# Four edits of hand-set order in a Fourier-mixing and ELU kernel: sums, products and a copy of the last step, and the steps of six sums per batch

## The chip, the core and the metric

The kernel runs on one core of a Trainium2 chip. The metric is the device time of one execution in microseconds (us); lower is better. The engines are TensorE (PE, matrix products; PEld is its weight load), VectorE (DVE), ScalarE (ACT), GpSimd (POOL) and SyncE (SP, which issues DMAs). Each engine works through its own queue in order, and engines wait for one another by semaphores.

## The reference

A two-dimensional Fourier transform of each batch, of which the real part goes through a two-layer network with an ELU between the layers.

```python
x: (8, 3008, 256) float32              # attention input
X = np.fft.fft(x, axis=1)
X = np.fft.fft(X, axis=2)
h = X.real.reshape(24064, 256) @ w_in  # w_in (256, 2048)
g = np.where(h > 0.0, h, np.exp(np.minimum(h, 0.0)) - 1.0)
out = g @ w_out                        # w_out (2048, 256), out (24064, 256)
```

## The kernel before

The transform over the rows is done on TensorE with constant cosine and sine matrices; the transform over the channels is folded into the first weight matrix. Because of the symmetry of the spectrum only half of the rows of each batch (1504) are transformed, as a cosine part (`Rr`) and a sine part (`Ir`); the sum and the difference of their products with the folded weights (`Wc` and `Ws`, both in `Wsc`) give a row and its mirror row. The 8 x 1504 = 12032 columns are cut into 47 tiles of 256 columns, each tile into 8 **steps** over the hidden width: 376 steps, 0 to 375. All data are float32; each product of the code (`mm`, L590) appears as two MATMUL instructions.

**One step** i does this. `mm_P` (PE, `H<-Rr,Wsc`) makes the cosine product in a PSUM bank `H`. `even_part` (DVE, L1339) reads it into `E`. `mm_Q` (PE, `H<-Ir,Wsc`) then adds the sine product into the same bank, so it has to wait for `even_part`. `h_minus` (DVE, L1353) makes the mirror row from `E` and `H`. `below_plus`, `below_minus`, `exp_plus`, `exp_minus` (ACT) and `g_plus`, `g_minus` (DVE, L1369) make the ELU: the results are blocks 0 and 1 (from `g_minus`) and 2 and 3 (from `g_plus`) of the buffer `G`. Four sums on POOL (L601), in this order, then make the operands of a seven-product scheme for the second layer: `sum_1` (block 5 = 2 - 3), `sum_3` (4 = 2 - 0), `sum_2` (2 = 5 - 0), `sum_4` (6 = 2 + 1). The second layer is `mm_X1` (`pA` from block 0; `pB` from block 1; then `pB` from the new block 2, with weights `WT`), `mm_X2` (`pC` from blocks 4 and 5) and `mm_X3` (`pD` from blocks 3 and 6).

**The order is written out by hand.** Each piece of work is entered with a due time (`at(t, fn)`, L1662). Slot k begins at k*T with T = 4.8 (`PERIOD`); the entries are sorted by due time and issued in that order, which is then the order of each engine's queue (`pin` keeps it). The due times are not times on the chip. Within a slot PE runs P of step k, X1 of step k-2, Q of step k, X2 and X3 of step k-2. In the first step of a tile X3 comes at the start of the following slot.

**Transforms of later batches** go in between: for batches b = 2 to 7, all entries of `rel(step, dt, ...)` (L1997) fall in slot r0 + step with r0 = 48*b - 70. `quarter_pairs` and `shift_pairs` (DVE) make sums and differences of row groups that the DFT products (`at_quarter`, L1968: two halves of products, `H<-QM,...`) take. `shift_pairs(b, ri, kodd, k)` (L876) issues two DVE instructions of 94x128 elements: with kodd = 1 two SCALAR_TENSOR_TENSOR (through `turn`, L870), with kodd = 0 two TENSOR_TENSOR (L598), all with both tensor inputs in SBUF. Their due time is 4.25 within the slot, which puts them behind `h_minus` and ahead of the `even_part` of the next slot on DVE.

**The last tile** (46) is combined from `pA` to `pD` on DVE in pieces: `comb_1` (u from `pA`, `pB`), a transpose, `comb_2` and `comb_22` (v and u with `pC`), a transpose, `comb_half` 0 (v with `pD`), a transpose, `comb_half` 1, a transpose. After each of the four transposes (L1527) `store` issues four DMAs of the result, two on the SP queue and two on the ACT queue (L1569). **The middle rows** (row 1504 of each batch) are done by themselves at the end: `mid_out` (PE, 16 small products, `H<-w,mid`), `mid_copy` (L1615, to SBUF), `mid_pick` (PE, one product that sums four groups), `mid_store` (DVE copy L1624 and one DMA on SP).

Of the kernel before, what the change touches and what calls it, by code (L numbers as in the profile page):

```python
# [15 lines left out]
ALU = mybir.AluOpType  # L16

SEQ = 3008
ND = 256
# [156 lines left out]
def kernel(  # L176
# [7 lines left out]
    nc = tc.nc  # L184
# [3 lines left out]
    n_tiles = (n_cols + TW - 1) // TW  # L188
# [17 lines left out]
    pin = tc.keep_in_program_order  # L206
# [393 lines left out]
    def gtt(o, a, b, op):  # L600
        pin(nc.gpsimd.tensor_tensor(out=o, in0=a, in1=b, op=op))  # L601

    def act(o, i, func=AF.Copy, **kw):
        pin(nc.scalar.activation(out=o, in_=i, func=func, **kw))  # L604
# [682 lines left out]
    def spread_ext(b, kodd):  # L1287
        for sl, a, z in ring_cut(b * HALF + kodd * RUN, RUN, False):
            a, z = a + kodd * RUN, z + kodd * RUN
            nc.sync.dma_start(  # L1290
                out=Rb[:, sl],
                in_=r128_dr[b : b + 1, a:z].to_broadcast([128, z - a]),
            )
            nc.sync.dma_start(out=Ir[127:128, sl], in_=r128_dr[b : b + 1, a:z])
# [68 lines left out]
    def exp_neg(ap):  # L1363
        act(ap, ap, func=AF.Exp, scale=-1.0)
# [33 lines left out]
    def blk(S, j, n=1):  # L1398
        return S.G[:, j * TW : (j + n) * TW]

    def sum_1(i):
        S = steps[i]
        gtt(blk(S, 5), blk(S, 2), blk(S, 3), ALU.subtract)

    def sum_3(i):
        S = steps[i]
        gtt(blk(S, 4), blk(S, 2), blk(S, 0), ALU.subtract)

    def sum_2(i):
        S = steps[i]  # L1410
        gtt(blk(S, 2), blk(S, 5), blk(S, 0), ALU.subtract)

    def sum_4(i):
        S = steps[i]
        gtt(blk(S, 6), blk(S, 2), blk(S, 1), ALU.add)

    def prod(i, a, half, lhsT, j):
        S, T = steps[i], tiles[i // 8]
# [18 lines left out]
    def mm_plain(i, a):  # L1437

        S = steps[i]
        q = i // 8  # L1440
        if i % 8 == 0 and a == 0:
            tiles[q] = Tile()
            tiles[q].acc = [bank(t) for t in ACC[2 * q : 2 * q + 2]]
        for n, (half, sign) in enumerate(((0, a), (1, 1 - a))):
            for r in range(2):
                mm(
                    tiles[q].acc[a][:, n * TW : (n + 1) * TW],
                    w2b(i, r, half),
                    blk(S, 2 * sign + r),
                    i % 8 == 0 and n == 0 and r == 0,  # L1450
                    i % 8 == 7,
                )
        if a:
            del steps[i]
# [158 lines left out]
            )  # L1613

    def mid_copy():  # L1615
        pin(nc.vector.tensor_copy(out=state["mh"][:, 0:ND], in_=state["mo"][:, 0:ND]))

    def mid_pick():
        po = state["mo"] = bank("H")
# [14 lines left out]
    state = {}  # L1634
# [27 lines left out]
    def at(t, fn):  # L1662
        events.append((t, len(events), fn))
# [69 lines left out]
    for slot in range(8):  # L1733
        i = slot % 2 * 8 + slot // 2
# [56 lines left out]
    T = PERIOD  # L1791
# [27 lines left out]
    for i in range(8):  # L1819
        at((12.9 + 0.5 * i) * T + 3.6, lambda i=i: sum_weights(i))  # L1820
    total = n_tiles * 8
    WINOGRAD = (
        (T + 2.91, sum_1),
        (T + 3.6, sum_3),
        (T + 4.4, sum_2),
# [4 lines left out]
    for slot in range(total):  # L1830
        i = slot % 2 * 8 + slot // 2 if slot < 16 else slot
        t = slot * T

        X3 = ((3 * T + 0.1 if i % 8 == 0 else 2 * T + 3.05, "", mm_X3),)
        for dt, key, fn in (
            (0.0, "P", mm_P),
            (0.9, "V", even_part),
            (2.17, "Q", mm_Q),
            (3.55, "h", h_minus),
            (4.2, "b+", below_plus),  # L1840
            (4.8, "b-", below_minus),
            (T + 0.01 if slot < 16 else T + 1.5, "x+", exp_plus),
            (T + 0.02 if slot < 16 else T + 2.21, "x-", exp_minus),
            (T + 2.2, "g+", g_plus),
            (T + 2.9, "g-", g_minus),
        ) + (
            (
                (2 * T + 0.87, "Xa", lambda i: mm_plain(i, 0)),
                (2 * T + 3.04, "Xb", lambda i: mm_plain(i, 1)),
            )  # L1850
            if i < 16
            else tuple((dt, "", fn) for dt, fn in WINOGRAD) + X3
        ):
            if f"{key}{slot}" not in front:
                at(t + dt, lambda fn=fn, i=i: fn(i))
# [28 lines left out]
    def safe(col):  # L1884

        return 8 * ((col - 1 - RING) // TW) + 8 if col > RING else 0
# [81 lines left out]
    def at_quarter(step, b, ri, kodd, finish, join):  # L1968
        box = []

        def d():
            if not box:
                box.append(Quarter(ri, b, kodd, state["Q", ri, kodd, b]))
            return box[0]

        def half(par):
            d().ps = bank("H")
            d().mms(par, d().ps)

        at(step * T + 4.75, lambda: half(0))  # L1980
        at((step + 1) * T + 0.9, lambda: d().copy())
        at((step + 1) * T + 1.0, lambda: d().unfold())
        at((step + 2) * T + 4.75, lambda: half(1))
        if kodd:
            at(finish * T + 4.26, lambda: d().finish())
            at((step + 3) * T + 0.9, lambda: d().copy_odd())
            at((step + 3) * T + 1.0, lambda: d().unfold_odd())
        assert join + 1 >= safe(b * HALF + (kodd + 1) * RUN)
        t = join * T + (4.25 if kodd else 1.01)
        at(t, lambda: d().plus())  # L1990
        at(t + 0.001, lambda: d().minus())

    for b in range(2, NB):
        s0 = (b - 1) * steps_b
        r0 = 48 * b - 70

        def rel(step, dt, fn, *key):  # L1997
            at((r0 + step) * T + dt, lambda: fn(*key))

        for far, rows in (  # L2000
            (0, ((0, 2, 0.2), (1, 2, 1.3), (3, 3, 0.2), (2, 5 if b == 2 else 3, 1.3))),
            (1, ((0, 27, 1.3), (1, 25, 0.2), (3, 28, 1.3), (2, 26, 3.0))),
        ):
            for j, n, dt in rows:
                rel(n, dt, load_quarter, b, j, far)
        for j, far, n, dt in (
            (0, 0, 4, 0.2), (3, 0, 4, 1.3), (1, 0, 5, 0.2), (2, 0, 6 if b == 2 else 5, 3.1),
            (1, 1, 27, 1.4), (2, 1, 28, 0.2), (0, 1, 29, 0.2), (3, 1, 30, 0.2),
        ):
            rel(n, dt, load_odd, b, j, far)  # L2010
        rel(4, 3.0, quarter_row, b)
        for far, start in ((0, 6), (1, 30)):
            for n in range(8):
                rel(start + n, 1.3, mirror_sum, (0, 3)[n % 2], far, (0, 2, 1, 3)[n // 2])
        for step, *key in (
            (13, 0, 0, 0), (20, 1, 0, 0), (21, 0, 0, 1), (22, 1, 0, 1),
            (35, 0, 1, 0), (36, 1, 1, 0), (37, 1, 1, 1), (38, 0, 1, 1),
        ):
            rel(step, 4.25, half_sum, *key)
        for step, *key in (  # L2020
            (14, 0, 0, 0), (21, 1, 0, 0), (23, 0, 0, 1), (25, 1, 0, 1),
            (38, 0, 1, 0), (40, 1, 1, 0), (42, 1, 1, 1), (44, 0, 1, 1),
        ):
            for ri in range(2):
                rel(step + ri, 1.3, channel_fold, ri, *key)
            kodd, far, h = key
            if h:
                rel(step, 4.0, channel_edge, kodd, far)
        for n in range(4):
            ri, m = divmod(n, 2)  # L2030
            rel(46 + n, 1.3, quarter_pairs, b, ri, 0, 1 + m)
        for n, step in enumerate((43, 44, 45, 46, 51, 53)):
            ri, m = divmod(n, 3)
            rel(step, 4.25, quarter_pairs, b, ri, 1, (2, 1, 3)[m])
        for step, *key in (
            (48, 0, 0, "u"), (49, 0, 1, "v"), (50, 1, 0, "v"), (52, 0, 1, "u"),
            (54, 1, 1, "u"), (56, 1, 1, "v"),
        ):
            rel(step, 4.25, shift_pairs, b, *key)
        for step, ri, kodd, finish, join in (  # L2040
            (51, 0, 0, 0, 54),
            (56, 1, 0, 0, 59),
            (59, 0, 1, 60, 75),
            (64, 1, 1, 66, 76),
        ):
            at_quarter(r0 + step, b, ri, kodd, r0 + finish, r0 + join)
        for kodd in range(2):
            step = s0 + (28, 38)[kodd]
            assert step >= safe(b * HALF + (kodd + 1) * RUN)
            at(step * T + 1.0, lambda b=b, kodd=kodd: spread_ext(b, kodd))  # L2050
# [5 lines left out]
    for n, dt, fn in (  # L2056
        (last, 4.75, mid_mm),
        (last + 1, 1.46, mid_below),
        (last + 2, 1.6, lambda: exp_neg(state["mr"])),
        (last + 3, 1.0, mid_g),  # L2060
        (total + 1, 3.3, mid_out),
        (total + 2, 2.9, mid_copy),
        (total + 2, 2.91, mid_pick),
        (total + 2, 2.92, mid_store),
    ):
        at(n * T + dt, fn)
# [32 lines left out]
```

## Time and profile before

| | |
|---|---|
| median of 3 runs | 1912.35 us (1911.55 to 1912.51) |
| profiled execution, its own time | 1911.92 us |
| span of the profiled execution, first to last instruction | 1910.1 us |
| granted TensorE clock | 1.000 |
| MATMUL instructions | 8972 |
| DVE, ACT, POOL busy | 1466.7, 876.9, 1352.6 us |

The profiled execution's time is 1.8 us more than its span, and 0.43 us below the median. A timeline line is: start, duration, engine, line of the kernel, operation, output<-inputs, shape, count, and in brackets the idle time before it with what ended it. The times of a merged line run from the first start to the last end. A queue's name ends in q (SPq, ACTq). A MATMUL lasts longer than the distance to the next one, since they are pipelined: two MATMULs of 128x256 start 0.216 us apart when nothing holds them, and 22 of them, a plain step, take 4.75 us.

### The profile page before, as it was taken

How to read it: one execution, taken by the hardware profiler on the slowest of the kernel's cores; microseconds unless marked ns; L12 is line 12 of the kernel's file. 1: busy time of each engine (PE TensorE's matmuls, PEld its weight loads, DVE VectorE, ACT ScalarE, POOL GpSimd, SP SyncE). 2: the span in 40 equal slices, each digit the busy share in tenths (PEclk: the TensorE clock that was granted, in tenths of full speed). 3: DMA queues.
4: the chain of work that ended last, by engine and by line, in shares of the span. 5: the costliest groups of instructions: out<-in, count | busy, mean ns of one | idle time of the engine just before them, and what ended most of it. 6: DMA issues, size and time to landing. Idle time of an engine off the chain costs nothing.

```text
span 1910.1 us, 27916 instructions
## 1 busy us (share of the span) xinstructions
PE 1901.3 (100%) x8972; PEld 1648.8 (86%) x8972; DVE 1466.7 (77%) x2786; ACT 876.9 (46%) x1710; POOL 1352.6 (71%) x1837
## 2 busy tenths in 40 slices
PE   9999999999999999999999999999999999999999
PEld 6888888888888888888888888888888888888887
DVE  8766667887778887778877787777877778767666
ACT  5754444444444444444444444444444444444443
POOL 4888667776677766777667776687766777556665
PEclk9999999999999999999999999999999999999999
DMA  8145212111011110111102111022110210000101
GB/s 339 45 33 43 57 24 47 50 25 35 12 45 41 32 33 12 46 40 30 31 19 49 35 27 29 13 55 44 24 24 16 55 20 16 17 12 15 20 12 23
DMA packets 278934, 73.80 MB, mean 39 GB/s; under 512 B 254402, under 2 KB 268998, under 8 KB 278788
## 3 DMA queue, kind: packets, MB, share of 16 engines
q1 hardware_dynamic: 270148, 61.58, 16.0%
q0 software_dynamic: 6464, 10.18, 1.7%
q8 instruction: 71, 1.16, 0.3%
q14 instruction: 75, 0.61, 0.1%
q10 hardware_dynamic: 2176, 0.26, 0.1%
HBM read 47.10 MB, written 24.80 MB: 38 GB/s over the span
## 4 chain that ended last, share of the span: by engine, by line
PE 96%; DVE 2%; DMA 0%; issue 0%; ACT 0%; POOL 0%; POOLq 0%; DVEq 0%
PE H L592 38%; PE pB L592 17%; PE pC L592 17%; PE pD L592 17%; PE pA L592 9%; DMA xl<-in_x_dram,ix 0%; DVE E L1339 0%; DVE e L689 0%; DVE o L689 0%; POOL w L601 0%; DVE G L1369 0%; DVE e L870 0%; DVE G L1353 0%; DVE Rr L598 0%; DVE pow L460 0%
## 5 line engine op out<-in xcount | busy, mean ns | idle before, releaser
L601 POOL TENSOR_TENSOR G<-G 128x256 f32<-128x256 f32 x1440 | 1049.3, 738 | 505.5 <-DVE G L1369 349.8
L604 ACT ACTIVATE G<-H 128x512 f32<-128x512 f32 x376 | 224.6, 597 | 931.5 <-DVE G L1353 927.9
L1339 DVE SCALAR_TENSOR_TENSOR E<-Rb,wex,H 128x256 f32<-128x256 f32 x752 | 327.5, 476 | 337.3 <-PE H L592 331.4
L592 PE MATMUL H<-Ir,Wsc 128*128 128x256 f32 x1504 | 388.1, 380 | 1.1 <-DVE E L1339 1.0
L592 PE MATMUL H<-Rr,Wsc 128*128 128x256 f32 x1504 | 387.6, 380 | 0.5 <-ACT Wsc L604 0.5
L592 PE MATMUL pC<-G,WT 128*128 128x256 f32 x1440 | 369.5, 379 | 0.0
L592 PEld LDWEIGHTS H<-Ir,Wsc 128*128 128x128 f32 x1504 | 277.7, 189 | 52.1 <-DVE E L1339 7.5
L592 PEld LDWEIGHTS H<-Rr,Wsc 128*128 128x128 f32 x1504 | 282.1, 190 | 41.6 <-issue 2.3
L592 PEld LDWEIGHTS pC<-G,WT 128*128 128x128 f32 x1440 | 273.6, 190 | 37.2
L1353 DVE SCALAR_TENSOR_TENSOR G<-E,H 128x512 f32<-128x512 f32 x376 | 257.0, 684 | 44.7 <-POOL G L601 11.4
L1369 DVE SCALAR_TENSOR_TENSOR G<-G,H 128x512 f32<-128x512 f32 x376 | 255.8, 680 | 37.9 <-ACT G L604 37.5
L1369 DVE SCALAR_TENSOR_TENSOR G<-M,G 128x512 f32<-128x512 f32 x376 | 256.7, 683 | 0.8 <-ACT M L604 0.8
L604 ACT ACTIVATE G<-G 128x512 f32<-128x512 f32 x376 | 233.3, 621 | 0.0
L592 PE MATMUL pB<-G,w 128*128 128x256 f32 x784 | 229.3, 379 | 0.0
L592 PE MATMUL pA<-G,w 128*128 128x256 f32 x784 | 229.3, 379 | 0.0
L592 PE MATMUL pD<-G,w 128*128 128x256 f32 x784 | 229.2, 379 | 0.0
L604 ACT ACTIVATE M<-G 128x512 f32<-128x512 f32 x376 | 223.9, 596 | 2.8 <-DVE G L1353 2.8
L604 ACT ACTIVATE M<-M 128x512 f32<-128x512 f32 x376 | 221.1, 588 | 0.1
L592 PE MATMUL pB<-G,WT 128*128 128x256 f32 x720 | 214.4, 379 | 0.0
L592 PE MATMUL pD<-G,WT 128*128 128x256 f32 x720 | 214.1, 379 | 0.0
L592 PEld LDWEIGHTS pA<-G,w 128*128 128x128 f32 x784 | 148.9, 190 | 20.5
L592 PEld LDWEIGHTS pB<-G,w 128*128 128x128 f32 x784 | 148.9, 190 | 20.4 <-PE H L592 0.2
(172 smaller groups left out, 1555.0 us busy)
## 6 DMA issues: line engine op xcount, KB each, us to landing
out_dram<-ot SPq DMA_DIRECT2D x496, 32.0 KB
xq<-in_x_dram SPq DMA_DIRECT2D x48, 94.0 KB
out_dram<-ot SPq DMA_DIRECT2D x256, 2.0 KB
Rb<-r SPq DMA_DIRECT2D x10, 376.0 KB
raw<-in_moe_w_in_dram SPq DMA_DIRECT2D x7, 512.0 KB
MC<-dft_mats SPq DMA_DIRECT2D x3, 943.5 KB
xq<-in_x_dram SPq DMA_DIRECT2D x12, 192.0 KB
xq<-in_x_dram SPq DMA_DIRECT2D x36, 64.0 KB
```

Of the source, the lines that this page charges most:

```text
L592: nc.tensor.matmul(out_, lhsT=lhsT, rhs=rhs, start=start, stop=stop, skip_group_check=True)
L601: pin(nc.gpsimd.tensor_tensor(out=o, in0=a, in1=b, op=op))
L604: pin(nc.scalar.activation(out=o, in_=i, func=func, **kw))
L1339: nc.vector.scalar_tensor_tensor(out=S.E[:, c], in0=Rb[:, cols(i)], scalar=wex[:, f : f + 1], in1=S.H[:, c], op0=ALU.mult, op1=ALU.add,)
L1353: nc.vector.scalar_tensor_tensor(out=two(S.G[:, 0:512])[:, :, ::-1], in0=two(S.E), scalar=2.0, in1=two(S.H), op0=ALU.mult, op1=ALU.subtract,)
L1369: nc.vector.scalar_tensor_tensor(out=o, in0=e, scalar=-1.0, in1=h, op0=ALU.add, op1=ALU.max)
```

## The change

Four edits.

1. In the last step (375) `sum_3`, `sum_2` and `sum_4` are put on VectorE; `sum_1` stays on GpSimd.
2. X3 of the last but one step (374) is put later: behind X2 of step 375 and ahead of X3 of step 375. The order of PE's second-layer products at the end was X1 X2 X3 (374), X1 X2 X3 (375) and becomes X1 X2 (374), X1 X2 (375), X3 (374), X3 (375).
3. The first copy of the middle rows is put on ScalarE, and its due time from 2.9 to 2.75. The transposes of the last tile are due at 2.4, 2.6 and 2.8 of the same slot, so that the copy now stands ahead of the last transpose and of its stores.
4. Four of the six `shift_pairs` entries of each batch from 2 to 7 are put in other slots, and with that change places: (0,1,u) from 52 to 50, (1,0,v) from 50 to 56, (1,1,u) from 54 to 58, (1,1,v) from 56 to 64.

```diff
+    def tt_of(i):
+
+        return vtt if i == n_tiles * 8 - 1 else gtt
+
...
     def sum_3(i):
         S = steps[i]
-        gtt(blk(S, 4), blk(S, 2), blk(S, 0), ALU.subtract)
+        tt_of(i)(blk(S, 4), blk(S, 2), blk(S, 0), ALU.subtract)
 
     def sum_2(i):
         S = steps[i]
-        gtt(blk(S, 2), blk(S, 5), blk(S, 0), ALU.subtract)
+        tt_of(i)(blk(S, 2), blk(S, 5), blk(S, 0), ALU.subtract)
 
     def sum_4(i):
         S = steps[i]
-        gtt(blk(S, 6), blk(S, 2), blk(S, 1), ALU.add)
+        tt_of(i)(blk(S, 6), blk(S, 2), blk(S, 1), ALU.add)
...
     def mid_copy():
-        pin(nc.vector.tensor_copy(out=state["mh"][:, 0:ND], in_=state["mo"][:, 0:ND]))
+        act(state["mh"][:, 0:ND], state["mo"][:, 0:ND])
...
-        X3 = ((3 * T + 0.1 if i % 8 == 0 else 2 * T + 3.05, "", mm_X3),)
+        X3 = (
+            (
+                3 * T + 0.1 if i % 8 == 0 else 3 * T + 3.045 if i == total - 2 else 2 * T + 3.05,
+                "",
+                mm_X3,
+            ),
+        )
...
         for step, *key in (
-            (48, 0, 0, "u"), (49, 0, 1, "v"), (50, 1, 0, "v"), (52, 0, 1, "u"),
-            (54, 1, 1, "u"), (56, 1, 1, "v"),
+            (48, 0, 0, "u"), (49, 0, 1, "v"), (50, 0, 1, "u"),
+            (56, 1, 0, "v"), (58, 1, 1, "u"), (64, 1, 1, "v"),
         ):
             rel(step, 4.25, shift_pairs, b, *key)
...
         (total + 1, 3.3, mid_out),
-        (total + 2, 2.9, mid_copy),
+        (total + 2, 2.75, mid_copy),
         (total + 2, 2.91, mid_pick),
         (total + 2, 2.92, mid_store),
```

## Prediction

> **What bounds the kernel now.** I read the engines' busy times first, then what PE's weight loads waited for, then the timeline of one batch's slots, then that of the end.
>
> ```profile
> PE 1901.3 (100%) x8972; PEld 1648.8 (86%) x8972; DVE 1466.7 (77%) x2786; ACT 876.9 (46%) x1710; POOL 1352.6 (71%) x1837
> ```
>
> PE is the bound over the whole span, so a shorter sum on another engine is worth nothing unless PE waited for it or it stands behind PE's last product. PE's own waits as the waits view counts them are small, but a busy MATMUL can hide a stall. Those of the weight loads show where to look:
>
> ```profile
> PEld H L592 <- DVE E L1339: 7.5, 19, 1.1
> ...
> PEld pB L592 <- POOL G L601: 0.8, 3, 0.4
> ```
>
> The first line is Q waiting for `even_part`, 19 times. To find what PE really lost I took the distance from each P product's start to the next (the length of a slot) over the whole run. It is 4.75 us in plain slots, and nearly everywhere a slot is longer by the DFT products in it alone. Two slots of each later batch are not. Here are slots r0+53 to r0+55 and r0+58 of batch 5 (r0 = 170), from the PE timeline:
>
> ```profile
> 1144.75 1.03 PE L592 MATMUL H<-Rr,Wsc 128*128 128x256 f32 x4
> ...
> 1150.77 1.03 PE L592 MATMUL H<-Rr,Wsc 128*128 128x256 f32 x4
> 1155.52 1.03 PE L592 MATMUL H<-Rr,Wsc 128*128 128x256 f32 x4
> 1160.59 1.03 PE L592 MATMUL H<-Rr,Wsc 128*128 128x256 f32 x4
> ```
> ```profile
> 1170.98 1.03 PE L592 MATMUL H<-Rr,Wsc 128*128 128x256 f32 x4
> ...
> 1176.81 1.03 PE L592 MATMUL H<-Rr,Wsc 128*128 128x256 f32 x4
> ```
>
> Slot 223 (r0+53) takes 6.02, slot 228 (r0+58) 5.83 with DFT products of the same shapes: 0.19 lost. Slot 225 (r0+55) has no DFT product and takes 5.07, not 4.75: 0.32 lost. Why, in slot 225:
>
> ```profile
> 1155.65 1.40 DVE L870 SCALAR_TENSOR_TENSOR e<-o,twist_tab,e 94x128 f32<-94x128 f32 x2
> 1156.98 0.85 DVE L1339 SCALAR_TENSOR_TENSOR E<-Rb,wex,H 128x256 f32<-128x256 f32 x2
> 1157.89 0.73 PEld L592 LDWEIGHTS H<-Ir,Wsc 128*128 128x128 f32 x4 [0.45 <-DVE E L1339]
> ```
>
> A scalar pair (`shift_pairs`) ends 1.53 us into the slot, `even_part` starts at 1.46, Q waits. The same happens in slot 223 (`even_part` at 1.33). In undisturbed slots it starts at 1.06 to 1.10, and at 1.14 (slot 220) PE still loses nothing. So the stall is the start of `even_part` less 1.14: 0.32 and 0.19, as found.
>
> The end of the run:
>
> ```profile
> 1898.46 0.68 DVE L1369 SCALAR_TENSOR_TENSOR G<-M,G 128x512 f32<-128x512 f32 x1
> 1898.69 3.02 POOL L601 TENSOR_TENSOR G<-G 128x256 f32<-128x256 f32 x4 [0.80 <-DVE G L1369]
> ...
> 1900.96 0.30 PEld L592 LDWEIGHTS pB<-G,WT 128*128 128x128 f32 x2 [0.37 <-POOL G L601]
> ...
> 1901.77 0.69 DVE L598 TENSOR_TENSOR u<-p,pB 128x512 f32<-128x512 f32 x1 [2.62 <-PE pB L592]
> ...
> 1905.93 0.39 DVE L1616 COPY mid<-H 128x256 f32<-128x256 f32 x1
> 1906.37 0.14 PEld L592 LDWEIGHTS H<-mid,pick 128*32 128x32 f32 x2 [1.61 <-DVE mid L1616]
> 1907.03 0.41 DVE L1624 COPY mid<-H 8x256 f32<-8x256 f32 x1 [0.71 <-PE H L592]
> 1907.47 0.29 SPq L1625 DMA_DIRECT2D out_dram<-mid  x1
> ```
>
> PE waits for the third sum of step 375; DVE starts the last tile when the third product of X1 is done and is then busy without a gap to the middle copy at 1905.93, although `mid_out` was done at 1905.25. That copy leads to the last DMA, which lands at 1908.91; the span ends 1.23 later with the closing waits.
>
> **What the Trainium skill says.** SBUF — State Buffer, Who interferes with whom: a VectorE instruction with two SBUF inputs contends with a GpSimd instruction that reads SBUF, the lock is exclusive for the whole instruction, and the first to start has it. The trace agrees: a pair's second instruction starts at 0.44 in slot 220 while a POOL sum runs from 0.34 to 1.07, and ends at 1.21, 0.14 after that sum. VectorE: DVE Perf Modes, "The TRN2 errata — SBUF-src ops pay a fixed extra latency per instruction": a float32 tensor_tensor of N elements takes (N+151)/0.96 ns, so 424 ns at 256; the trace has 422 (e<-xl 128x256, nothing on POOL). DMA: Bandwidth & Descriptors, Issuing engines are not separate DMA queues: several issuing engines save only the sequencer's time of issue. Here a store occupies the ACT queue for 0.44 (median), which counts for edit 3.
>
> **The change part by part.** *Scalar pairs (edit 4).* No instruction is added. The six batches' lengths of slot r0+53 are 6.018, 6.022, 6.026, 6.020, 6.020, 6.025 against 5.833: 1.13 us over. Those of r0+55 are 4.935, 4.939, 5.068, 5.065, 4.935, 4.941 against 4.749: 1.39 over (the 5.07s are batches whose joins wrap in the ring buffer, two DVE pieces more). Sum 2.52. The pairs due in 52 and 54 ran at the head of 53 and 55; both go. Nothing else is late there: in slot 52 `h_minus` ends at 4.87 of 4.78, in slot 54 at 4.97 of 4.75, so `even_part` then waits for P alone, at about 1.06.
>
> Where they land. Slot 50 loses a TENSOR_TENSOR pair and gets a scalar pair. The nearest row is the scalar pair due in 49: it starts at 4.5, its second instruction sits out a POOL sum and ends at 1.20 to 1.22, `even_part` starts at 1.13 to 1.146; cost nothing in five batches, 0.006 in the sixth. In 51 POOL's sum begins 0.04 earlier, so I take 0; bounds 0 and 0.05 per batch. Slot 56 loses a scalar pair for a plain one: shorter, 0. In slot 58 DVE is free after the transpose at 4.59 of 5.83, so the pair ends about 0.03 into slot 59, a full us early: 0. Slot 64 has the same DVE order as slot 56 (`h_minus` ends at 4.65, as at 4.66), where a scalar pair ended at 1.07 and `even_part` started at 1.09, on time: 0, bounds 0 and 0.1 per batch, since POOL's sums may fall otherwise. The DFT halves that read the pairs are two slots later or more; (1,0,v) and (1,1,v) are nearest, due in 56 and 64 and read by products due at 58 and 66 + 4.75. No DMA moves. Body: -2.52 (-2.6 to -1.6).
>
> *Sums on VectorE, product order (1, 2).* `g_minus` ends at 1899.14, `sum_1` on POOL at 1899.42. `sum_3` waits for the lock: 0.14 after POOL's end for 128 elements, so some 0.28 for 256, end 1899.70. `sum_2` then takes 0.42 alone, less up to 0.08 by which neighbours on DVE overlap: 1900.04 to 1900.15, where POOL had ended it at 1900.91. `sum_4` follows by 1900.55. On DVE nothing waits behind these three until `comb_1`. On PE, X3(374) is four MATMULs, 0.86, so X1(375) could start at 1899.10 in place of 1899.96; now it meets `g_minus` at 1899.20 and loses 0.2 (the stall before shows 0.1 for an exposed weight load besides the wait). Its third product would be due at 1900.17 and gets its operand at 1900.10 to 1900.20 and its weights 0.1 later: 0.04 to 0.14 lost. Together 0.25 to 0.35, against 0.25 lost before, so PE ends `mid_out` at 1905.25 to 1905.34: no gain on PE. But the third product and all that DVE makes of it comes 0.8 earlier (1900.42 to 1900.52 in place of 1901.28 for its second MATMUL): `comb_1` at about 1900.97. `comb_half` 0 would come at 1903.56 and the last `pD` is ready at 1903.5 to 1903.6: no wait worth counting. The last transpose ends at 1905.21.
>
> *Copy on ScalarE (3).* A 128x256 copy from PSUM takes 0.384 there (p<-pA), as on DVE. Ahead of it on the ACT queue stand the stores of the third transpose. They were issued until 1906.36, the queue being full from 1904.47 on; 0.8 earlier is 1905.56. So the copy starts at 1905.61, later than `mid_out` allows, and ends at 1906.0; `mid_pick` starts at 1906.05 in place of 1906.37. Gain 0.32 to the last DMA. The last two ACT stores start behind the copy, at about 1905.65 instead of 1906.455, and land first. Bounds: 0.7 if the queue doesn't hold the copy, -0.1 if the sums take the lock worse or DMA traffic holds the stores.
>
> **Sum.** 1911.92 - 2.52 - 0.32 = 1909.08 on the profiled execution, which lies 0.43 below the median; against the median 1912.35 - 2.84 = **1909.5**.
>
> **Rivals.** (A) The end gains nothing: the copy is held by the stores or `mid_out` is later. For it: ACT's queue is full; against: it fills 0.8 earlier. 1909.8 or up to 1910.0. (B) Larger gain at the end and no hold on ACT, 0.7: 1909.1; and if the run scatters by another 0.6 as the three runs did by 0.96 in all, over 0.2% is just reached. (C) A scalar pair in slot 50 or 64 makes a new stall: each at the 0.32 seen in slot 225, 2 x 6 x 0.32 = 3.84, and the kernel is slower: 1912.35 - 2.84 + 3.84 = 1913.3. It decides from 0.24 per pair on, that is `even_part` at 1.38. Against it: the two nearest pairs give 1.146 and 1.09. (D) The stalls in 53 and 55 stay, because something else on DVE or `mm_Q`'s operand was last: then only the end, 1912.0. Against: the two slots' DVE timelines have no other instruction between.
>
> **How the numbers follow.** Forecast 0.68, A 0.12, B 0.10, C 0.06, D 0.04. A measurement of this kernel can tell about 0.2%, 3.8 us, from no change. All of the likeliest cases are within it: faster by more 0.12 (half of B, and a tenth of the forecast by scatter), slower by more 0.03 (half of C: with the pair in 58 held too, or dearer), within 0.85. Range 1908.5 to 1911.0: the body's bounds (-2.6 to -1.6), the end's (-0.7 to +0.1) and half a us of scatter.
>
> **What would show it.** Slots r0+53 at 5.83 and r0+55 at 4.75 in all six batches; r0+51, r0+59 and r0+65 as long as before (5.61, 5.62, 5.64); 12 fewer waits of PEld for E. At the end: `comb_1` about 0.8 earlier against the end of PE's products, `mid_pick` 0.3 earlier, the ACT copy right behind two stores. Wrong if `even_part` starts after 1.14 in r0+51 or r0+65, or if a total over 3.8 us appears, which no stall of before would explain.

## The result, and the profile after

| | before | after |
|---|---|---|
| median | 1912.32 us (22 runs, 1911.21 to 1917.64) | 1909.65 us (22 runs, 1908.40 to 1911.34) |
| profiled execution's span | 1910.1 us | 1907.7 us |

The ratio is 0.9985, 95% interval 0.9979 to 0.9992: 2.7 us less, within the 0.2% (3.8 us) that was named as the bound of "no change", where 1909.5 had been forecast. A comparison over this many runs does tell it from 1.

The busy times of the page:

```profile
PE 1899.9 (100%) x8972; PEld 1649.8 (86%) x8972; DVE 1466.4 (77%) x2788; ACT 877.1 (46%) x1711; POOL 1348.9 (71%) x1834
```

The work is the same: 8972 MATMULs, three sums moved from POOL to DVE, one copy from DVE to ACT. What changed is waiting. Waits of PE's weight loads, changed kernel (total us, times, longest):

```profile
PEld H L592 <- DVE E L1339: 3.4, 7, 1.1
...
PEld pB L592 <- DVE G L598: 0.4, 1, 0.4
PEld pA L592 <- DVE G L1369: 0.3, 1, 0.3
```

The waits for `even_part` fell from 19 to 7: the twelve of slots r0+53 and r0+55, two in each of six batches, are gone. The two last lines are new, and lie in the last step.

PE's timeline, slots 223 to 226, which hold r0+53 and r0+55 of batch 5 (first MATMULs of P):

```profile
1143.98 1.03 PE L592 MATMUL H<-Rr,Wsc 128*128 128x256 f32 x4
1149.81 1.03 PE L592 MATMUL H<-Rr,Wsc 128*128 128x256 f32 x4
1154.56 1.03 PE L592 MATMUL H<-Rr,Wsc 128*128 128x256 f32 x4
1159.31 1.03 PE L592 MATMUL H<-Rr,Wsc 128*128 128x256 f32 x4
```

Slot 223 takes 5.83 and slot 225 takes 4.75, where they took 6.02 and 5.07. In slot 225 `even_part` now waits for P alone, and Q's weight load, the last line, has no wait for `even_part` any more:

```profile
1154.10 0.68 DVE L1353 SCALAR_TENSOR_TENSOR G<-E,H 128x512 f32<-128x512 f32 x1
...
1155.63 0.87 DVE L1339 SCALAR_TENSOR_TENSOR E<-Rb,wex,H 128x256 f32<-128x256 f32 x2 [0.85 <-PE H L592]
1156.55 0.79 PEld L592 LDWEIGHTS H<-Ir,Wsc 128*128 128x128 f32 x4
```

The end of the run, all engines:

```profile
1896.65 0.72 POOL L601 TENSOR_TENSOR G<-G 128x256 f32<-128x256 f32 x1 [0.80 <-DVE G L1369]
1897.14 1.51 DVE L598 TENSOR_TENSOR G<-G 128x256 f32<-128x256 f32 x3
1897.16 0.30 PEld L592 LDWEIGHTS pA<-G,w 128*128 128x128 f32 x2 [0.34 <-DVE G L1369]
...
1898.24 0.30 PEld L592 LDWEIGHTS pB<-G,WT 128*128 128x128 f32 x2 [0.35 <-DVE G L598]
...
1899.05 0.69 DVE L598 TENSOR_TENSOR u<-p,pB 128x512 f32<-128x512 f32 x1 [0.40 <-PE pB L592]
...
1900.25 3.40 ACTq L1574 DMA_DIRECT2D out_dram<-ot  x6
...
1902.85 0.45 DVE L1531 STREAM_TRANSPOSE ot<-v 128x256 f32<-128x256 f32 x1
1903.69 0.38 ACT L604 ACTIVATE mid<-H 128x256 f32<-128x256 f32 x1 [5.41 <-DMA out_dram<-ot]
...
1904.79 0.41 DVE L1628 COPY mid<-H 8x256 f32<-8x256 f32 x1 [1.49 <-PE H L592]
1905.23 0.29 SPq L1629 DMA_DIRECT2D out_dram<-mid  x1
```

X1 of the last step waits for `g_minus` and then for `sum_2`, which is now on DVE. DVE is through with the last transpose at 1903.30, and the copy on ACT starts only at 1903.69: the bracket names the stores, whose issues (the ACTq line) hold ScalarE's queue until 1903.65, and not `mid_out`.

**Where the time went.** The distances from P to P cancel what differs between executions at the start. The twelve slots r0+53 and r0+55 are 2.52 us shorter together (each by what it lost before), no slot of the others named in the prediction moved by over 0.005, and from the last step's first P product to the end of the span it is 0.38 us less (17.95 to 17.57). Slots outside the change (18 and 106) make 0.16. They scatter between the profiles: slot 106 took 3.97 or 3.89 in kernels with edit 4 and in kernels without it. The spans differ by 2.4 and not by 3.1, since in the later profile the first P product came 0.65 later after the first instruction. That start lay between 26.2 and 28.1 us in the profiles of this study, whatever the kernel, so the slots are a sharper measure here than the spans.

### The profile page after: what moved, and what is told of

It reads as the page before. It is cut to its first block, busy times and chain, and to the rows that moved or that the text cites. A ratio compares the mean times of both kernels' runs of the same rounds, so it can differ in the third digit from the quotient of the medians.

```text
span 1907.7 us, 27911 instructions
## 1 busy us (share of the span) xinstructions
PE 1899.9 (100%) x8972; PEld 1649.8 (86%) x8972; DVE 1466.4 (77%) x2788; ACT 877.1 (46%) x1711; POOL 1348.9 (71%) x1834
## 4 chain that ended last, share of the span: by engine, by line
PE 97%; DVE 2%; DMA 0%; issue 0%; ACT 0%; POOL 0%; ACTq 0%; POOLq 0%; DVEq 0%
PE H L592 38%; PE pB L592 17%; PE pC L592 17%; PE pD L592 17%; PE pA L592 9%; DMA xl<-in_x_dram,ix 0%; DVE e L689 0%; DVE o L689 0%; POOL w L601 0%; DVE E L1339 0%; DVE pow L460 0%; DVE w L418 0%; DVE v L598 0%; DVE u L598 0%; ACT Wsc L604 0%
```

## The experiments

The theory: a scalar pair ahead of `even_part` delays Q by the start of `even_part` less 1.14 us into the slot, because the pair sits out POOL's sums; nothing else in the body counts, and the end is a small sum of its own. The rivals: the end carries the gain; the slots hold too much DVE work, in whatever order; a pair's own length is the cost.

**Edit 4 alone.**

```diff
-            (48, 0, 0, "u"), (49, 0, 1, "v"), (50, 1, 0, "v"), (52, 0, 1, "u"),
-            (54, 1, 1, "u"), (56, 1, 1, "v"),
+            (48, 0, 0, "u"), (49, 0, 1, "v"), (50, 0, 1, "u"),
+            (56, 1, 0, "v"), (58, 1, 1, "u"), (64, 1, 1, "v"),
```

> The kernel before with edit 4 alone (scalar pairs in other slots). Order theory (what counts is whether a pair stands ahead of even_part late enough to hold Q): slots r0+53 and r0+55 fall to 5.83 and 4.75 in all six batches, 2.52 us less in the body, the end unchanged (17.9 us from the last step's first P product to the end of the span): ratio 0.9987. Rival, that the end's edits carry the gain: no change, 1.0000.

Median 1910.63, ratio 0.9988 (0.9981 to 0.9994). The twelve slots lost 2.52, the end stayed at 17.93. The body's gain is this edit's.

**Edits 1 to 3 alone**, the list of pairs as before.

> The kernel before with edits 1 to 3 alone (sums, product order, copy). Order theory: the body keeps its 2.52 us of stalls, the end is 0.38 us shorter as in the changed kernel (17.5 us from the last step's first P to the end): ratio 0.9998. Rival, that the end's edits carry the gain: 2.4 to 2.9 us less, 0.9986.

Median 1912.20, ratio 1.0000 (0.9991 to 1.0008); slots r0+53 and r0+55 of the six batches kept their lengths within 0.012 us, the end is 17.57 us. The rival is out: it needed 0.9986. That the end's 0.38 us shortens the run is read from the trace alone; no timing here could show it.

**The same pairs in the same slots, behind `even_part`.**

```diff
-            (48, 0, 0, "u"), (49, 0, 1, "v"), (50, 1, 0, "v"), (52, 0, 1, "u"),
-            (54, 1, 1, "u"), (56, 1, 1, "v"),
+            (48, 0, 0, "u"), (49, 0, 1, "v"), (50, 1, 0, "v"), (56, 1, 1, "v"),
         ):
             rel(step, 4.25, shift_pairs, b, *key)
+        for step, *key in (
+            (53, 0, 1, "u"), (55, 1, 1, "u"),
+        ):
+            rel(step, 0.95, shift_pairs, b, *key)
```

> The kernel before; the scalar pairs (0,1,u) and (1,1,u) run in the same slots r0+53 and r0+55 as before, but behind even_part and not ahead of it. Order theory: even_part starts at 1.06 to 1.10 in these slots and both stalls go, 2.5 us less, ratio 0.9987, with the same DVE work in the same slots. Rival, that these slots hold too much DVE work: slots stay at 6.02 and 4.94 to 5.07, 1.0000, or the stall goes to the following slot.

Somewhat over half of it came, as the slots show; the time alone (median 1910.92, ratio 0.9993, 0.9985 to 1.0001) is not told from no change. Both slots lost their whole stall, 2.52 us together, but slot r0+56 grew by 0.16 in three batches, by 0.30 and 0.28 in two and not at all in the last, 1.07 us in all. Timeline of batch 5, slots 225 and 226:

```profile
1156.24 0.87 DVE L1339 SCALAR_TENSOR_TENSOR E<-Rb,wex,H 128x256 f32<-128x256 f32 x2 [0.85 <-PE H L592]
1157.03 1.21 DVE L870 SCALAR_TENSOR_TENSOR e<-o,twist_tab,e 94x128 f32<-94x128 f32 x2
...
1159.96 0.67 DVE L598 TENSOR_TENSOR u<-p,pB 128x512 f32<-128x512 f32 x1
1160.74 0.69 DVE L598 TENSOR_TENSOR v<-u,pC 128x512 f32<-128x512 f32 x1
1161.34 0.86 DVE L1339 SCALAR_TENSOR_TENSOR E<-Rb,wex,H 128x256 f32<-128x256 f32 x2
...
1162.26 0.73 PEld L592 LDWEIGHTS H<-Ir,Wsc 128*128 128x128 f32 x4 [0.41 <-DVE E L1339]
```

In slot 225 Q waits for nothing. The pair behind `even_part` pushes the rest of DVE's slot, `comb_1` and `comb_2` of the tile come in front of the next `even_part`, and that one is late, at 1.42 into slot 226, where the slot lost 0.28. So order decides in slot r0+53, and in r0+55 the rival is right: from there to r0+56 DVE has too much to do in five of the six batches, and the pair has to leave, as it did in the change.

**Two pairs ahead of one `even_part`.**

```diff
-            (54, 1, 1, "u"), (56, 1, 1, "v"),
+            (54, 1, 1, "u"), (54, 1, 1, "v"),
```

> The kernel before; the scalar pair (1,1,v) is due in slot r0+54 too, so that two pairs stand ahead of one even_part, none in 56. Order theory with the price found, stall = start of even_part less 1.14: the second pair ends 2.7 to 3.0 us into slot r0+55, even_part starts at 2.6 to 2.95, and the slot grows from 4.94 to 5.07 to 6.2 to 6.6, 7 to 9 us more in all, ratio 1.0037 to 1.0047. Rival, that a pair costs a set 0.19 to 0.32 us wherever it stands ahead of even_part: 1.1 to 1.9 us more, 1.0006 to 1.0010.

Median 1920.82, ratio 1.0047 (1.0033 to 1.0060). Timeline of batch 5, slot 225, which begins at 1160.19:

```profile
1159.36 3.03 POOL L601 TENSOR_TENSOR G<-G 128x256 f32<-128x256 f32 x4 [3.29 <-DVE G L1369]
...
1160.19 1.03 PE L592 MATMUL H<-Rr,Wsc 128*128 128x256 f32 x4
1160.32 2.94 DVE L870 SCALAR_TENSOR_TENSOR e<-o,twist_tab,e 94x128 f32<-94x128 f32 x4
1162.34 0.78 POOL L601 TENSOR_TENSOR xq<-xq,xq 96x255 f32<-96x255 f32 x1
1163.19 0.86 DVE L1339 SCALAR_TENSOR_TENSOR E<-Rb,wex,H 128x256 f32<-128x256 f32 x2
...
1164.10 0.73 PEld L592 LDWEIGHTS H<-Ir,Wsc 128*128 128x128 f32 x4 [1.99 <-DVE E L1339]
```

`even_part` starts 3.00 us into the slot; less 1.14 that is 1.86, and the slot took 6.60, 1.85 more than a plain one. The price per late microsecond is one, up to a delay six times as long as before. The slots grew by 8.85 us in all; a set price per pair would have given 1.1 to 1.9.

**No POOL sums beside the late pairs.** The pairs stay where they were; the sums of 12 steps are left out, and one ScalarE copy per step fills their blocks with other data, so that this kernel leaves a part of the computation out.

```diff
+    bare = {48 * b - 70 + n for b in range(2, NB) for n in (51, 53)}
+
+    def gsum(i, o, a, b, op):
+        if i not in bare:
+            gtt(o, a, b, op)
...
     def sum_1(i):
         S = steps[i]
-        gtt(blk(S, 5), blk(S, 2), blk(S, 3), ALU.subtract)
+        if i in bare:
+            act(blk(S, 4, 3), blk(S, 0, 3))
+        gsum(i, blk(S, 5), blk(S, 2), blk(S, 3), ALU.subtract)
...
```

> The kernel before, with the scalar pairs where they were; in steps r0+51 and r0+53 of the six batches (12 of 376 steps) the four sums are left out, and one ScalarE copy of blocks 0 to 2 to blocks 4 to 6 stands in for them, so POOL is not reading SBUF while the late pairs run. Lock theory (a pair takes 1.40 us because its instructions sit out POOL's sums): the pair takes 0.7 to 0.8 us, even_part starts at 1.06 to 1.14 in slots r0+53 and r0+55, which take 5.83 and 4.75: 2.5 us less. Rival, that the pair's own length is the cost: slots 6.02 and 4.94 to 5.07 as before, time 1912.3.

One run, 1909.74; slots r0+53 and r0+55 lost 2.52 us, as in the change. In the kernel before, POOL's sums ran right through the pair of slot 225 (1155.65 to 1157.05):

```profile
1154.68 3.03 POOL L601 TENSOR_TENSOR G<-G 128x256 f32<-128x256 f32 x4 [3.30 <-DVE G L1369]
```

Without them, the same slot of batch 5:

```profile
1154.55 0.72 DVE L870 SCALAR_TENSOR_TENSOR e<-o,twist_tab,e 94x128 f32<-94x128 f32 x2
1155.49 0.87 DVE L1339 SCALAR_TENSOR_TENSOR E<-Rb,wex,H 128x256 f32<-128x256 f32 x2 [0.21 <-PE H L592]
1156.41 0.79 PEld L592 LDWEIGHTS H<-Ir,Wsc 128*128 128x128 f32 x4
```

The pair takes 0.72 instead of 1.40, at the same place in the slot, and `even_part` waits for P. The stall was POOL's sums in the way of a pair, not the pair's own length.

**The end, edit by edit.** Four kernels; what they measured stands in one table below. Edits 1, 2 and 4 (the copy on VectorE again):

```diff
-        act(state["mh"][:, 0:ND], state["mo"][:, 0:ND])
+        pin(nc.vector.tensor_copy(out=state["mh"][:, 0:ND], in_=state["mo"][:, 0:ND]))
...
-        (total + 2, 2.75, mid_copy),
+        (total + 2, 2.9, mid_copy),
```

> The changed kernel without edit 3: the first copy of the middle rows is on VectorE again, behind the last transpose. Times from the last step's first P product. If ScalarE's queue of stores holds the copy (it starts at 13.54 there, the second store of the third transpose ends at 13.49, mid_out ends at 13.1), the copy on VectorE starts at 13.1 to 13.15 as soon as the last transpose ends (13.14), mid_pick 0.4 earlier, and the end comes 0.2 to 0.4 us earlier than in the changed kernel (17.1 to 17.3, not 17.54). Rival, that edit 3 is worth 0.2 or more: the end is later, 17.7.

Edit 1 alone, edit 2 alone and edit 3 alone, each as in the change's diff:

> The kernel before with edit 1 alone (three sums of the last step on VectorE). Times from the last step's first P product. sum_2 ends at 8.03 as in the changed kernel, before X1's third product is due (8.6), so PE's 0.25 us stall goes and comb_1 starts at 9.33 in place of 9.57; mid_out ends 0.25 earlier; the chain on VectorE and the end come 0.25 earlier: 17.67 in place of 17.92. If the end is set by the stores and not by this chain: 17.9.

> The kernel before with edit 2 alone (X3 of step 374 behind X2 of step 375). Times from the last step's first P product. X1's third product still waits for sum_2 on POOL until 8.77, so comb_1 starts at 9.57 as before; PE has the 0.86 us of X3(374) still to do then and loses it at the wait, mid_out ends 0.8 to 0.9 later at 13.9, comb_half 0 waits for pD (about 12.3 to 12.4 in place of 12.17), the copy starts at 13.9 or a little later in place of 13.74: the end 0.1 to 0.3 later, 18.0 to 18.2. Rival, that the order alone brings comb_1 0.7 forward: 17.5.

> The kernel before with edit 3 alone (copy on ScalarE). Times from the last step's first P product. The copy stands behind two stores of the third transpose, whose second ends at 14.17, and so starts at 14.2 in place of 13.74: mid_pick and the last DMA are 0.4 to 0.5 later; the end 0.2 to 0.5 later, 18.1 to 18.4. Rival, that ScalarE takes the copy as soon as mid_out is done (13.1): the end 0.4 earlier, 17.5.

Times in us from the last step's first P product, from the same profiles (a start, except where it says end):

```
edits        comb_1  mid_out  middle  mid_pick  last DMA  last DMA  end of
                     end      copy              issued    landed    span
none           9.57   13.06    13.74    14.18     15.28     16.72    17.95
1              9.33   12.82    13.51    13.95     15.05     16.46    17.69
2              9.57   13.92    13.99    14.46     15.56     16.84    18.07
3              9.57   13.06    14.22    14.65     15.75     17.02    18.25
1, 2, 4        8.90   13.25    13.32    13.79     14.89     16.17    17.39
1, 2, 3, 4     8.90   13.24    13.54    13.97     15.07     16.34    17.57
```

Edit 1 alone ends 0.25 earlier: `sum_2` is there before X1's third product is due, and PE's stall goes. Edit 2 alone ends 0.12 later: its room in front of X1 is spent on waiting for POOL, and PE does X3(374) afterwards. With edit 1, edit 2 brings a further 0.30 (17.69 to 17.39). They are worth more together than apart, since `sum_2` on POOL ended at 8.71, when PE in its old order was due to use it at 8.63: with either of the two left as it was, X1's third product could not start before 8.63. The expectation for edit 2 was wrong in one point: `comb_half` 0 started at 12.17, as before; it didn't wait.

Edit 3 alone ends 0.31 later, and put on top of 1 and 2 it ends 0.18 later (17.39 to 17.57). ScalarE's queue is why; its lines and VectorE's in the kernel with edit 3 alone (all engines):

```profile
1903.59 3.40 ACTq L1570 DMA_DIRECT2D out_dram<-ot  x6
...
1906.19 0.45 DVE L1527 STREAM_TRANSPOSE ot<-v 128x256 f32<-128x256 f32 x1
1907.04 0.38 ACT L604 ACTIVATE mid<-H 128x256 f32<-128x256 f32 x1 [5.43 <-DMA out_dram<-ot]
```

Six stores take the queue to 1906.99 and the copy starts 0.05 after; DVE was free at 1906.64. With edits 1 and 2 but not 3, the copy stands behind the last transpose on VectorE and waits for `mid_out` alone:

```profile
1906.95 0.45 DVE L1531 STREAM_TRANSPOSE ot<-v 128x256 f32<-128x256 f32 x1
1907.56 0.42 DVE L1620 COPY mid<-H 128x256 f32<-128x256 f32 x1 [0.17 <-PE H L592]
```

The end of 17.39 fell short of the expected 17.1 to 17.3 because `mid_out` ended at 13.25 and not at 13.1; the changed kernel's trace had it at 13.24 already, so the expectation started from a wrong figure. The times of this kernel are 1910.48 in the median of 20 runs, ratio 0.9989 (0.9982 to 0.9996): not to be told from the change's. Its profiled execution also showed a wait that has nothing to do with the edits (waits of PE):

```profile
PE H L592 <- POOL xe L601: 2.4, 1, 2.4
```

In slot 29 PE waited for data that small loads on SP's queue bring; the slot took 9.60 us, 6.86 in the other profiles.

**Those loads due one slot earlier**, with the copy on VectorE.

```diff
-            (14.4 + 0.5 * n) * T,
+            (13.4 + 0.5 * n) * T,
```

> The changed kernel without edit 3, and with the 16 small loads of one channel (load_ext) due one slot earlier each, so that the data of the DFT in slot 29 lands about 4.8 us earlier on SP's queue. Order theory: body as in the changed kernel (slots r0+53 and r0+55 at 5.83 and 4.75), end 17.39 as with the copy on VectorE, slot 29 at 6.86 in every profile; median 1909.4 and fewer executions over 1912: ratio 0.9986. Rival, that the earlier loads hold up SP's other loads (weights for slots 13 to 20): slots 14 to 26 longer, no gain over 1909.65.

No gain: median 1910.15 of 21 runs, ratio 0.9989 (0.9982 to 0.9995), with one execution above 1912 us (1914.5), where four of 20 were with the loads at their old due time and none of 22 in the changed kernel; so few don't show a difference. The end is 17.38 as expected, and slot 29 took 6.86, as in every profile but that one. The last of the reads that depend on these loads was issued at 181.6 us, when it was 180.0 in the changed kernel: the earlier due time of the loads did not bring it forward. The rival didn't show either: slots 14 to 26 were together 0.03 us longer than in the changed kernel. Two slots outside the edits (294 and 370) were 0.29 and 0.11 longer than before in this profile; in slot 294 `even_part` started at 1.57 in place of 1.28, which is the same 0.29. Why it was late there stays open. No version was shown to beat the changed kernel; by the trace, leaving edit 3 out is worth 0.18 us, a hundredth of a per cent.

## Why the prediction was right

**Body.** Right in place and size: 1.13 and 1.39 us were forecast for slots r0+53 and r0+55, and the slots gave 1.13 and 1.39. That the pairs cost nothing where they landed held to 0.005 us per slot, in r0+51, r0+57, r0+59 and r0+65. The rule used, start of `even_part` less 1.14, was found at 0.19 and 0.32 and held at 1.86. It also accounts for two slots that the forecast passed over, 106 and 294, where `even_part` started at 1.22 and 1.28 in the kernel before and the slots lost 0.09 and 0.14. The cause of the long pair was argued from one pair's times and from the Trainium skill (SBUF — State Buffer, Who interferes with whom), which has a VectorE instruction with two SBUF inputs contend with a GpSimd instruction that reads SBUF. The run without the sums shows that POOL's sums are the cause: 0.72 us for the pair in place of 1.40. That it is a lock held to the end of an instruction is the page's statement; the traces agree, since both instructions of the pair in slot 225 ended 0.14 us after a POOL sum.

**Sums and order.** The right mechanism, with some terms off. `sum_3` ended at 7.50 after the last P (7.51 forecast). `sum_2` was taken to overlap its neighbour and end by 7.96; it started 0.10 after `sum_3`, with a semaphore instruction between, and ended at 8.03. PE's two stalls came to 0.43 against 0.25 to 0.35, and `comb_1` 0.68 earlier against 0.8. `mid_out` ended 0.18 later than before, 0 to 0.09 forecast.

**Copy.** The forecast said rightly that the queue of stores would hold the copy until they were out; it came 0.12 later than forecast, with the chain that it hangs on, and the last DMA was issued 0.21 earlier in place of 0.32. The span gained 0.38 all the same: that DMA landed 1.27 after its issue, 1.44 before, a term the sum did not have. So it was luck that the total at the end came near the forecast 0.32. The shorter landing comes from the longer distance to the stores ahead. The kernel with edit 2 alone shows it: its stores were issued as before (within 0.01 us), the last DMA 0.28 later, and it landed 1.28 after its issue. With edit 1 alone, where all of them moved forward together, it took 1.41. What the sum called the gain of edit 3 came from edits 1 and 2; the forecast did not ask what the copy would do on VectorE, which would have shown it free sooner.

**Rivals.** C and D fell with the changed kernel's own slots: no new stall, none left. A's end without gain and B's of 0.7 lie on either side of the 0.38. The time of 1909.65 lies between the forecast 1909.5 and A's 1909.8 and can't tell them apart; the trace of the end does. B's is out of reach since ACT did hold the copy, and without that hold it was 0.56. The stated range ended at 1911.0; its own terms add up to 1911.35, which changes nothing here.

## What to carry to other kernels

Measure the distance between two equal marks of the bound engine along the whole run: a tenth of a microsecond lost in a slot shows there while the engine counts as 100% busy. An instruction ahead of the one that the bound engine waits for costs what it makes that one late, microsecond for microsecond, and nothing below the slack; so ask what holds it up (here another engine's sums) and in which slots there is room, since the same work moved behind can be late again one slot on. Before work is given to an idle engine, read its queue: DMA issues fill one without counting as busy.

## What had not been expected

Waiting for a POOL sum cost each 94x128 instruction of a pair between 0.24 and 0.42 us (0.59 and 0.77 against 0.35 alone), more than its own length in the second. The three sums on VectorE, of which the second overwrites an input of the first and the third reads the result of the second, did not overlap: they took 0.52, 0.43 and 0.43 us and started 0.62 and 0.46 apart. And two edits at the end, of which one alone lost 0.12 and the other gained 0.25, gave 0.56 together.
